# The opening of an attention and mixer kernel, rebuilt: v loaded straight into its rows, one head's scores by the ordinary product, two AV products moved among the scores

## The chip, the cores and the metric

The kernel runs on one core of a Trainium2 chip. The metric is device time in microseconds (us), the median of several runs. The core's engines each run their own list of instructions in order and wait for one another by semaphores: PE (matrix products; its weight loads are shown as PEld), DVE (VectorE), ACT (ScalarE), POOL (GpSimd) and SP (SyncE). POOL and SP issue the DMA transfers here: POOL those that also change float32 to bfloat16, SP the rest.

## The reference

q, k and v have shape 8 batches x 8 heads x 576 positions x 64, s has 8 x 8 x 576. Each head is causal attention with a bias from the running sum of the positive part of s; its output x then goes through a low-rank mixer over positions (U, V of rank 32) and a two-layer mixer over channels.

```python
scores = scale * np.matmul(q, k.transpose(0, 1, 3, 2))
cum = np.cumsum(np.maximum(s, 0.0), axis=-1)
bias = -(cum[:, :, :, None] - cum[:, :, None, :])
scores = np.where(causal, -1e9, scores + np.minimum(bias, 0.0))
attn = np.exp(scores - np.max(scores, axis=-1, keepdims=True))
attn = attn / (np.sum(attn, axis=-1, keepdims=True) + 1e-09)
x = np.matmul(attn, v)          # then heads side by side: 8 x 576 x 512
u = x + (x.T @ U @ V).T         # per batch, over positions
out = u + np.maximum(u @ w_ch1, 0.0) @ w_ch2
```

## The kernel before

**Units of work.** Heads go in pairs: 32 pairs, four to a batch. A pair has these steps, each a Python generator whose pieces the order written at the end of the kernel calls one by one with `step`:

- `transposes(n)`, T: PE turns q and k of both heads (`q_sd`, `k_sd`) into PSUM tiles (L317); `copies` (L291) says for each head and half whether ACT or DVE copies them into `slot` (L340), where head and position stand crosswise. A slot has 64 rows of q or k and four rows more, the bias rows, which a DMA on SP fills (L233 for batch 0, L301 later): the cumulative sum in three bfloat16 parts, and ones. So one product of slot with slot gives score plus bias.
- `scores(n)`, S: for each head a "near" tile of 128x1024 (six matmuls, L404) and one exponential on ACT (L419) into `pT`; then one "mid" tile for both heads (L430) and one small "tail" tile (L436). The near, mid and tail pieces together are the causal half of the 576x576 scores. PSUM holds two such large tiles (`pscore`) and four of 128x512 (`pwork`).
- masks on the diagonal blocks: in batch 0 POOL does three for each pair (L152).
- `values(n)`, V (AV): 15 matmuls for each head (L464) with v from `v_slot`, whose 65th column of ones gives the sum of each row, then on DVE a reciprocal (L473) and a product (L474) into `x_sb`.
- `mix_first`, M: the low-rank mixer of batch 0, for each of four blocks of 128 channels: five matmuls with `U_sb` (L598), DVE copy to `ux_first` (L601), then four transposing matmuls and one with `V_sb` (L605, L613), ACT to `uT` (L621). Then comes the first channel product (L650), with the first half of w1.

**The first batch.** Two things are special at the start. First, near scores of pair 0 do not wait for the bias rows in slot 0: `near_by_rows` (L358) builds score and bias in PSUM from the row tile itself with 27 matmuls on 64 rows (L366), in four pieces, and does it for both heads (generators `A` and `B_`). Second, batch 0's v comes as one DMA in long runs, four positions to a partition (`v_raw`, L167, 512 KB in bfloat16), and `v_tiles` (L575) brings it into order by 16 matmuls with a selecting matrix `sel` and four DVE casts (L590); the last 64 positions come straight (L188). `spin` (L216) issues matmuls on a constant tile whose result nobody reads; they keep PE at work.

**What sets the order.** PE and POOL run in the order in which the kernel is written; so do DVE, ACT and SP up to the end of batch 0 (`in_program_order`). POOL's DMA issues share eight semaphores in turn, so an issue waits for the landing of the eighth before it, and the queue carries them in the order of issue. The order of the opening stands in lines 1098 to 1168: spins, T0, A, T1, pieces of `B_` between T2, then S0, T3, S1, masks, S2 with `v_tiles` inside, S3 with V0 in its midst, V1, M, V2, M, V3, M.

On POOL the order is: q and k of batch 0 in four pieces each, `sel`, `keep` (a constant mask used from batch 1 on), v, memsets of `v_slot`, the end of v, memsets of U_sb and V_sb, U, U, V (L262 to L266), first half of w1 (L270), masks of pair 0, first four heads of batch 1's q and k, memsets of the ones in pT, masks of pair 1, second half of w1, and so on.

Of the kernel before, what the change touches and what calls it, by code (L numbers as in the profile page):

```python
# [39 lines left out]
def kernel(  # L40
# [52 lines left out]

    PW = 1664
    v_early = work.tile([128, NF, 512], BF16, tag="hT", name="hT").rearrange("p a b -> p (a b)")
    v_raw = v_early[:, 0:2048].rearrange("p (h t d) -> p h t d", h=H, t=4)
# [27 lines left out]
    def ones(ap):  # L124
# [10 lines left out]
    load_qk(0, 4, 2)  # L135
    load_qk(0, 6, 2)

    sel = consts.tile([128, 516], BF16)
    nc.vector.memset(sel, 0.0)
    nc.gpsimd.affine_select(  # L140
        out=sel,
        in_=sel,
        compare_op=ALU.not_equal,
        fill=1.0,
        base=-3,
        pattern=[[1, 516]],
        channel_multiplier=-4,
    )
# [16 lines left out]
    nc.gpsimd.memset(keep, 3.0e38)  # L165
    causal(keep, 1, 128)
    nc.gpsimd.dma_start(  # L167
        out=v_raw.rearrange("p h t d -> p h (t d)"),
        in_=v[0, :, 0:512, :].rearrange("h (p t) d -> p h (t d)", t=4),
    )  # L170

    v_slots = [consts.tile([128, 5, H, D + 1], BF16, name=f"v_slot{i}") for i in range(3)]

    def init_v(eng, vt):
# [6 lines left out]

    def load_v(b, parts=range(5)):
        vt = v_slot(b)
        if b < 3:
            init_v(nc.gpsimd, vt)
        for t in parts:
            rows_t = 128 if t < 4 else 64
            nc.gpsimd.dma_start(  # L188
                out=vt[:rows_t, t, :, 0:D],
                in_=v[b, :, ds(t * 128, rows_t), :].rearrange("h p d -> p h d"),  # L190
            )

    load_v(0, [4])
    nc.gpsimd.memset(U_sb, 0.0)
    nc.gpsimd.memset(V_sb, 0.0)

    pTs = [consts.tile([128, 2, PW], BF16, name=f"pT{i}") for i in range(2)]

# [12 lines left out]

    for slot in slots:
        nc.vector.memset(slot[:KA, :, 2 * S :], 0.0)


    def spin(n, dst):  # L216
# [12 lines left out]
    nc.vector.tensor_copy(rows[:, 1, 1, :], rest)  # L229
    nc.vector.tensor_sub(rows[:, 2, 1, :], rest, rows[:, 1, 1, :])  # L230
    for n in range(PB):
        for hh in range(2):
            nc.sync.dma_start(  # L233
                out=slots[n][D:KA, hh, 0 : 2 * S],
                in_=rows[2 * n + hh : 2 * n + hh + 1].rearrange("n r c s -> n r (c s)"),
            )
# [16 lines left out]
    def weight_sums():  # L253
        for dst, a, b in ((B_1, B12, B11), (B_2, B22, B_1), (B_4, B21, B_2), (B_3, B22, B12)):
            for k4 in range(0, HF, 4):
# [6 lines left out]
    nc.gpsimd.dma_start(  # L262
        out=U_sb[:, :4, 0:R], in_=moe_U[:512].rearrange("(kt kp) r -> kp kt r", kp=128)
    )
    nc.gpsimd.dma_start(out=U_sb[:64, 4, 0:R], in_=moe_U[512:576])
    nc.gpsimd.dma_start(out=V_sb[:R], in_=moe_V)  # L266
    w1_in = moe_w_ch1.rearrange("(kt kp) n -> kp kt n", kp=128)

    def load_w1(half):
        nc.gpsimd.dma_start(  # L270
            out=w1_sb[:, :, ds(half * 1024, 1024)], in_=w1_in[:, :, ds(half * 1024, 1024)]
        )
# [5 lines left out]
        )  # L278

    load_w1(0)  # L280
    alloc_qk(1)
    uT_of, x_of, xT_of = {}, {}, {}

# [6 lines left out]

    def copies(n, hh, par):  # L291
        b = n // PB
        on_act = hh == (n == 4) and ((n in (0, 1, 4, 8, 9) or n > 8 and n % PB == 2) or n == 2 and par == 0)
        return nc.scalar.copy if on_act else nc.vector.tensor_copy

    def transposes(n):
        b, hp = divmod(n, PB)
        slot = slot_of(n)
        if b > 0:
            for r, n_r, c in ((0, 3, 1), (3, 1, 0)):  # L300
                nc.sync.dma_start(  # L301
                    out=slot[ds(D + r, n_r), :, ds(c * S, S)],
                    in_=rows_hbm[ds(r, n_r), ds(2 * n, 2)],
                )
        tps = {}

        def turn(hh, c):
            if c == 0:
                tile = pwork()
                if (n, hh) == (3, 0):  # L310
                    spin(2, tile)
                tps[hh] = tile.bitcast(BF16)[:, : 2 * 4 * TP].rearrange(
                    "p (c t m) -> p c t m", c=2, t=4
                )
            src = (q_t[b], k_t[b])[c]
            for t2 in range(4):
                nc.tensor.transpose(  # L317
                    tps[hh][:, c, t2, :],
                    src[:, 2 * hp + hh, ds(t2 * 128, 128)],
                    identity[:TP, :TP],  # L320
                )

        if b == 0:
            for hh in range(2):
                turn(hh, 0)
            yield
        for hh in range(2):
            if b > 0:
                turn(hh, 0)
            turn(hh, 1)  # L330
            tp = tps[hh]
            dst = slot[0:D, hh, 0 : 2 * S]
            for par in range(2):
                src = tp[par * D : par * D + D]
                if in_runs(b, 2 * hp):
                    by_run = dst.rearrange("p (c t two m) -> p c t two m", c=2, t=4, two=2)
                    copies(n, hh, par)(by_run[:, :, :, par, :], src)  # L337
                else:
                    in_turn = dst.rearrange("p (c m t two) -> p c m t two", c=2, t=4, two=2)
                    copies(n, hh, par)(  # L340
                        in_turn[:, :, :, :, par], src.rearrange("p c t m -> p c m t")
                    )
            yield
# [53 lines left out]
        nc.scalar.activation(pT[:, hh, 0:1024], near, EXP, scale=scale)  # L397
        yield

    def scores(n, pT, spins=()):  # L400
        slot = slot_of(n)

        def mm(dst, hh, j, lo, hi):
# [5 lines left out]
                stop=True,  # L409
            )  # L410

        tail = None
        for hh in range(2) if n > 0 else ():
            near = pscore()
            for j in range(4):
                mm(near[:, ds(j * 128, 128)], hh, j, j * 128, j * 128 + 128)
            mm(near[:, 512:960], hh, 0, 128, S)
            mm(near[:, 960:1024], hh, 3, 512, S)
            nc.scalar.activation(pT[:, hh, 0:1024], near, EXP, scale=scale)  # L419
            if n >= PB:  # L420
                mask(pT[:, hh, 0:512].rearrange("p (a b) -> p a b", a=4), 4, 128)
            if spins:
                tail = tail or pwork()
                spin(spins[hh], tail)
            yield
        mid, tail = pscore(), tail or pwork()
# [144 lines left out]
        evac(slice(0, 4), 512, S, ut)  # L571
        yield


    def v_tiles():  # L575
        vt = v_slots[0]
        pvs = [pwork() for _ in range(4)]
        spin(2, pvs[0])
        yield
        for t in range(4):  # L580
            for j, pv in enumerate(pvs):
                nc.tensor.matmul(
                    pv.rearrange("p (h d) -> p h d", h=H),
                    lhsT=sel[ds(32 * j, 32), ds(3 + 128 * j - t, 128)],
                    rhs=v_raw[ds(32 * j, 32), :, t, :],
                    start=(t == 0),
                    stop=(t == 3),
                )
        for j, pv in enumerate(pvs):
            nc.vector.tensor_copy(vt[:, j, :, 0:D], pv.rearrange("p (h d) -> p h d", h=H))  # L590

    ux_first = work.tile([128, PB, 128], BF16, tag="ux_first", name="ux_first", bufs=1)

# [496 lines left out]
    def step(*gens):  # L1090
        for gen in gens:
            next(gen, None)
# [2 lines left out]
        spin(n, (ps or pscore)()[:, 0:512])  # L1095

    act, dve = nc.scalar.copy, nc.vector.tensor_copy
    S0, S1, S2, S3 = (scores(n, pT_of(n), {1: (2, 3), 3: (2, 0)}.get(n, ())) for n in range(PB))
    T0, T1, T2, T3 = (transposes(n) for n in range(PB))
    M0, M1, M2, M3 = (mix_first(dt, act) for dt in range(PB))  # L1100
    A, B_ = (near_by_rows(hh, pT_of(0)) for hh in range(2))
    spin_some(9)
    step(T0)
    spin_some(2)
    step(T0, T0)
    step(A, A, A, A)
    step(T1, T1, T1)
    step(B_)
    step(T2)
    step(B_)  # L1110
    step(T2, T2)
    step(B_, B_)
    step(S0, S0)
# [201 lines left out]
```

## Time and profile before

| what | value |
|---|---|
| time, median of 3 runs | 363.95 us (363.31 to 364.02) |
| span of the profiled execution | 362.1 us |
| time less that span | 1.85 us |
| PE busy | 350.2 us (97%) |
| DVE busy | 276.5 us (76%) |
| ACT busy | 213.0 us (59%) |
| POOL busy | 84.7 us (23%) |
| first 30 us: PE, DVE, ACT, POOL busy | 27.30, 23.51, 19.34, 27.09 us |
| chain that ended last: PE, DVE, ACT, DMA | 76%, 11%, 4%, 4% |

A line such as "13.54 1.02 ACT L397 ..." in a timeline has start and length in us, engine, line of the kernel, operation, tiles, shape and count; brackets tell how long the engine was idle before and what ended it. The chain that ended last is followed back from the end; in order of time it lists start, length and what ran. A DMA row ends with the us from issue to landing. The stages list for each stretch the busy time of PE, PEld, DVE, ACT and POOL, the granted clock of PE as a share, the busy share of the DMA engines (over 1 where several transfers overlap on an engine) and GB/s.

### The profile page before, as it was taken

To read this page: it belongs to the slowest core of one execution; us is meant where nothing else is said; L and a number is where in the kernel's file an instruction comes from. 1 tells how busy PE (TensorE), PEld (TensorE's weight loads), DVE (VectorE), ACT (ScalarE), POOL (GpSimd) and SP (SyncE) were. 2 spreads that over 40 slices of the span, in tenths; PEclk is the share of its full clock that TensorE was granted. 3 is DMA by queue.
4 is the path that set the end of the run, shared out by engine and by line. 5 is a ranking of instruction groups with operands and counts; after the bars stand their busy time and mean duration, and the time that the engine had idled before them with its cause. 6 is when DMAs were issued, how large, how long until landed. Compare 5 with 4: busy or idle time off the path is not lost.

```text
span 362.1 us, 9616 instructions
## 1 busy us (share of the span) xinstructions
PE 350.2 (97%) x3999; PEld 256.7 (71%) x4039; DVE 276.5 (76%) x605; ACT 213.0 (59%) x322; POOL 84.7 (23%) x108
## 2 busy tenths in 40 slices
PE   8999999999998999999999999999899999999996
PEld 3676566665587667876688667876488548888885
DVE  8776776778788758995699659986697769676674
ACT  3875975846761678347843676348743554675710
POOL 8997261714040403140214013000000000000000
PEclk9999999999999999999999999999999999999999
DMA  7999999999999899969994999255022716010022
GB/s 104 169 198 204 150 174 129 152 150 143 98 109 114 147 121 70 97 94 126 128 91 72 127 150 91 51 123 79 4 38 70 143 24 125 29 60 31 30 89 87
DMA packets 155123, 37.94 MB, mean 105 GB/s; under 512 B 138696, under 2 KB 153448, under 8 KB 155080
## 3 DMA queue, kind: packets, MB, share of 16 engines
q0 software_dynamic: 110016, 18.50, 82.6%
q1 hardware_dynamic: 44776, 18.64, 31.4%
q8 instruction: 31, 0.51, 0.6%
q10 hardware_dynamic: 288, 0.20, 0.2%
q14 instruction: 12, 0.10, 0.1%
HBM read 37.25 MB, written 9.70 MB: 130 GB/s over the span
## 4 chain that ended last, share of the span: by engine, by line
PE 76%; DVE 11%; ACT 4%; DMA 4%; issue 3%; POOL 1%; DVEq 0%; ACTq 0%; POOLq 0%
PE pwork L650 21%; PE pwork L699 11%; PE pscore L404 9%; PE quarter L699 9%; PE pwork L464 7%; PE parts L929 6%; PE pwork L317 4%; PE pwork L660 3%; DMA xT<-x_sb 2%; DVE slot L677 2%; DVE uT L518 2%; ACT hT L1018 2%; DVE o_sb L713 2%; DMA k_sd<-in_k_dram 2%; ACT pT L419 1%
## 5 line engine op out<-in xcount | busy, mean ns | idle before, releaser
L650 PE MATMUL pwork<-uT,w_sb 128*128 128x512 bf16 x401 | 105.9, 379 | 2.6 <-ACT hT L1018 0.9
L1018 ACT ACTIVATE hT<-pwork 128x512 bf16<-128x512 f32 x108 | 65.2, 608 | 38.4 <-PE pwork L650 38.2
L419 ACT ACTIVATE pT<-pscore 128x1024 bf16<-128x1024 f32 x56 | 56.5, 1029 | 49.8 <-PE pscore L404 49.0
L650 PEld LDWEIGHTS <-w_sb 128*128 128x128 bf16 x448 | 38.3, 98 | 35.9 <-issue 1.3
L404 PE MATMUL pscore<-slot 68*128 68x320 bf16 (+1 forms) x500 | 55.2, 246 | 0.2
L404 PEld LDWEIGHTS <-slot 68*128 68x128 bf16 x564 | 41.2, 97 | 16.9 <-issue 1.3
L699 PEld LDWEIGHTS <-hT 128*128 128x128 bf16 x496 | 46.3, 98 | 7.0 <-DVE uT L518 0.5
L188 POOL DMA_DIRECT2D v_slot<-in_v_dram x36 | 30.3, 855 | 77.6 <-PE pwork L464 65.9
L349 DVE TENSOR_TENSOR pT<-pT,keep 128x512 bf16<-128x512 bf16 (+1 forms) x81 | 28.6, 354 | 21.8 <-ACT pT L419 16.0
L337 DVE COPY slot<-pwork 64x576 bf16<-64x576 bf16 x76 | 34.4, 453 | 4.6 <-PE pwork L317 3.7
L464 PEld LDWEIGHTS <-pT 128*128 128x128 bf16 x870 | 32.4, 98 | 6.9 <-issue 1.8
L464 PE MATMUL pwork<-v_slot,pT 128*128 128x65 bf16 x870 | 35.5, 193 | 1.2 <-DVE uT L518 1.2
L474 DVE TENSOR_TENSOR x_sb<-pwork,rec 128x320 bf16<-128x320 f32 x64 | 31.2, 488 | 1.4
L430 ACT ACTIVATE pT<-pscore 128x1024 bf16<-128x1024 f32 x29 | 30.2, 1043 | 1.7 <-PE pscore L404 1.5
L699 PE MATMUL pwork<-w_sb,hT 128*128 128x256 bf16 x240 | 30.6, 273 | 0.0
L340 DVE COPY slot<-pwork 64x576 bf16<-64x576 bf16 x29 | 23.3, 802 | 5.4 <-PE pwork L317 3.6
L699 PEld LDWEIGHTS <-slot 128*128 128x128 bf16 x256 | 24.1, 98 | 4.6 <-issue 1.6
L114 POOL DMA_DIRECT2D q_sd<-in_q_dram x6 | 12.6, 2105 | 47.2 <-PE pwork L317 34.5
L473 DVE RECIPROCAL rec<-pwork 128x5 f32<-128x5 f32 x64 | 12.0, 190 | 12.3 <-PE pwork L464 12.1
L699 PE MATMUL pwork<-w_sum,slot 128*128 128x256 bf16 x160 | 20.3, 272 | 0.7 <-DVE o_sb L713 0.7
L317 PEld LDWEIGHTS <-q_sd 72*128 72x128 bf16 x256 | 14.7, 98 | 8.8 <-DMA q_sd<-in_q_dram 1.0
L699 PE MATMUL quarter<-w_sb,hT 128*128 128x256 bf16 x144 | 18.0, 273 | 0.3 <-DVE uT L518 0.3
(165 smaller groups left out, 544.4 us busy)
## 6 DMA issues: line engine op xcount, KB each, us to landing
out_dram<-o_sb SPq DMA_DIRECT2D x34, 256.0 KB
w_sb<-in_moe_w_ch_dram POOLq DMA_DIRECT2D x4, 1024.0 KB, 14.3
v_slot<-in_v_dram POOLq DMA_DIRECT2D x28, 128.0 KB, 8.3
q_sd<-in_q_dram POOLq DMA_DIRECT2D x5, 576.0 KB, 15.6
k_sd<-in_k_dram POOLq DMA_DIRECT2D x5, 576.0 KB, 21.8
q_sd<-in_q_dram POOLq DMA_DIRECT2D x4, 288.0 KB, 13.2
k_sd<-in_k_dram POOLq DMA_DIRECT2D x4, 288.0 KB, 13.5
q_sd<-in_q_dram POOLq DMA_DIRECT2D x4, 144.0 KB, 5.2
```

What stands on the lines that cost most here:

```text
L188: nc.gpsimd.dma_start(out=vt[:rows_t, t, :, 0:D], in_=v[b, :, ds(t * 128, rows_t), :].rearrange("h p d -> p h d"),)
L317: nc.tensor.transpose(tps[hh][:, c, t2, :], src[:, 2 * hp + hh, ds(t2 * 128, 128)], identity[:TP, :TP],)
L337: copies(n, hh, par)(by_run[:, :, :, par, :], src)
L349: nc.vector.tensor_tensor(dst, dst, keep[:, :, 0:w].to_broadcast([128, n_tiles, w]), op=ALU.min)
L404: nc.tensor.matmul(dst, lhsT=slot[0:KA, hh, ds(S + j * 128, 128)], rhs=slot[0:KA, hh, lo:hi], start=True, stop=True,)
L419: nc.scalar.activation(pT[:, hh, 0:1024], near, EXP, scale=scale)
L430: nc.scalar.activation(pT[:, :, 1024:1536], mid.rearrange("p (a b) -> p a b", a=2), EXP, scale=scale)
L464: nc.tensor.matmul(po[:, i, :], lhsT=pT[:, hh, ds(place(j, i), 128)], rhs=vt[:, j, h, :], start=(j == 0), stop=(j == i), skip_group_check= ...
L474: nc.vector.tensor_tensor(x_sb[:, hp, :, ds(hh * D, D)], po[:, :, 0:D], rec.to_broadcast([128, 5, D]), op=ALU.mult,)
L650: nc.tensor.matmul(f1, lhsT=w1_sb[:, kt, ds(nf * 128, 128)], rhs=u[:, kt, :], start=(kt == 0), stop=(kt == 3),)
L699: nc.tensor.matmul(acc[:, i, :], lhsT=a[:, kt, ds(i * 128, 128)], rhs=b[:, kt, :], start=(begin and i == 0 and kt == 0), stop=(kt == HF - ...
L1018: nc.scalar.activation(hT[:, nf, :], f1, RELU)
```

## The change

- Batch 0's v is loaded like every other batch's: five DMAs straight into `v_slot` (four of 128 positions and one of 64, runs of 64 numbers). `v_raw`, `sel` and `v_tiles` go. The memsets of this v slot move from POOL to DVE.
- `near_by_rows` is kept for the first head of pair 0. The second head's near scores come from `scores(0)`, by six matmuls on slot 0 with its bias rows; the DMA of these rows is issued before that of the first head's.
- U, U and V of the mixer and the mask `keep` are issued after the masks of pair 0 (`load_mixers`), behind the first half of w1; memsets of U_sb, V_sb and of the ones in pT stand between w1 and the masks. The first q and k of batch 1 come after the masks of pair 1.
- The order: S0's three pieces directly after T1, T2 after it in one go; T3 in three pieces between S1, S2 and V0; V0 inside S2, V1 and the first M piece inside S3.
- One of two copies of pair 1's first head goes to DVE, and the one of pair 2 on ACT too. Spins stay in two places only: at the start and two ahead of S0.

```diff
-    nc.gpsimd.dma_start(
-        out=v_raw.rearrange("p h t d -> p h (t d)"),
-        in_=v[0, :, 0:512, :].rearrange("h (p t) d -> p h (t d)", t=4),
-    )
...
-        if b < 3:
+        if 0 < b < 3:
             init_v(nc.gpsimd, vt)
...
-    load_v(0, [4])
-    nc.gpsimd.memset(U_sb, 0.0)
-    nc.gpsimd.memset(V_sb, 0.0)
...
+    init_v(nc.vector, v_slots[0])
+    load_v(0)
...
-        for hh in range(2):
+        for hh in (1, 0) if n == 0 else range(2):
             nc.sync.dma_start(
                 out=slots[n][D:KA, hh, 0 : 2 * S],
...
     load_w1(0)
+    for pT in (*pTs, pT_early[0]):
+        nc.gpsimd.memset(pT[:, :, 1600:], 1.0)
+    nc.gpsimd.memset(U_sb, 0.0)
+    nc.gpsimd.memset(V_sb, 0.0)
+
+    def load_mixers():
+        nc.gpsimd.dma_start(
+            out=U_sb[:, :4, 0:R], in_=moe_U[:512].rearrange("(kt kp) r -> kp kt r", kp=128)
+        )
+        nc.gpsimd.dma_start(out=U_sb[:64, 4, 0:R], in_=moe_U[512:576])
+        nc.gpsimd.dma_start(out=V_sb[:R], in_=moe_V)
+        nc.gpsimd.memset(keep, 3.0e38)
+        causal(keep, 1, 128)
...
-        on_act = hh == (n == 4) and ((n in (0, 1, 4, 8, 9) or n > 8 and n % PB == 2) or n == 2 and par == 0)
+        on_act = hh == (n == 4) and (
+            n in (0, 4, 8, 9) or n > 8 and n % PB == 2 or n == 1 and par == 0
+        )
...
-        for hh in range(2) if n > 0 else ():
+        for hh in range(n == 0, 2):
             near = pscore()
+            spin(spins[hh], near[:, 0:512])
...
     step(A, A, A, A)
     step(T1, T1, T1)
-    step(B_)
-    step(T2)
-    step(B_)
-    step(T2, T2)
-    step(B_, B_)
-    step(S0, S0)
-    step(T3, T3, T3)
-    step(S1)
+    step(S0, S0, S0)
     masks(pT_of(0), True)
-    load_qk(1, 0, 4)
-    for pT in (*pTs, pT_early[0]):
-        nc.gpsimd.memset(pT[:, :, 1600:], 1.0)
-    step(S1)
+    load_mixers()
+    step(T2, T2, T2)
+    step(S1, S1)
+    step(T3)
+    step(T3)
     step(S1, S1)
     masks(pT_of(1), True)
+    load_qk(1, 0, 4)
     nc.gpsimd.memset(slots[PB][D:KA, :, 0 : 2 * S].bitcast(mybir.dt.uint32), 0x3F803F80)
     load_w1(1)
-    step(S2)
-    vs = v_tiles()
-    step(vs)
-    step(S2)
-    drain(vs)
-    step(S2)
-    step(S3)
-    step(S2)
+    step(S2, S2)
+    step(V0, V0)
+    step(T3)
+    step(S2, S2)
     masks(pT_of(2), True)
     nc.gpsimd.memset(pT_early[1][:, :, 1600:], 1.0)
     step(S3)
-    drain(values(0, pT_of(0)))
+    step(V1, V1)
+    step(S3)
+    step(M0)
     step(S3, S3)
     masks(pT_of(3), True)
-    drain(values(1, pT_of(1)))
     load_qk(1, 4, 4)
     load_w2(0)
     nc.gpsimd.memset(V_end, 0.0)
-    step(M0)
-    drain(values(2, pT_of(2)))
+    step(V2, V2)
     step(M0, M1)
-    drain(values(3, pT_of(3)))
+    step(V3, V3)
     step(M1, M2)
```

More of the change, by code (lines that the diff above doesn't have):

```diff
@@ L95 @@
     v_early = work.tile([128, NF, 512], BF16, tag="hT", name="hT").rearrange("p a b -> p (a b)")
-    v_raw = v_early[:, 0:2048].rearrange("p (h t d) -> p h t d", h=H, t=4)
     pT_early = [
@@ L136 @@
     load_qk(0, 6, 2)
[L138 to L147, printed above, removed]
-    )
     keep = consts.tile([128, 1, 128], BF16)
@@ L164 @@
     V_end = consts.tile([128, 4, 64], BF16)
-    nc.gpsimd.memset(keep, 3.0e38)
-    causal(keep, 1, 128)
-    nc.gpsimd.dma_start(
-        out=v_raw.rearrange("p h t d -> p h (t d)"),
-        in_=v[0, :, 0:512, :].rearrange("h (p t) d -> p h (t d)", t=4),
-    )
     v_slots = [consts.tile([128, 5, H, D + 1], BF16, name=f"v_slot{i}") for i in range(3)]
@@ L261, in weight_sums @@
                 yield
[L262 to L266, printed above, removed]
     w1_in = moe_w_ch1.rearrange("(kt kp) n -> kp kt n", kp=128)
@@ L309, in turn @@
                 tile = pwork()
-                if (n, hh) == (3, 0):
-                    spin(2, tile)
                 tps[hh] = tile.bitcast(BF16)[:, : 2 * 4 * TP].rearrange(
@@ L398, in near_by_rows, with scores @@
         yield
-    def scores(n, pT, spins=()):
+    def scores(n, pT, spins=(0, 0)):
         slot = slot_of(n)
@@ L410, in mm @@
             )
-        tail = None
-        for hh in range(2) if n > 0 else ():
+        for hh in range(n == 0, 2):
             near = pscore()
+            spin(spins[hh], near[:, 0:512])
             for j in range(4):
@@ L421, in scores @@
                 mask(pT[:, hh, 0:512].rearrange("p (a b) -> p a b", a=4), 4, 128)
-            if spins:
-                tail = tail or pwork()
-                spin(spins[hh], tail)
             yield
-        mid, tail = pscore(), tail or pwork()
+        mid, tail = pscore(), pwork()
         for hh in range(2):
@@ L572, in seqmix @@
         yield
[L575 to L590, printed above, removed]
     ux_first = work.tile([128, PB, 128], BF16, tag="ux_first", name="ux_first", bufs=1)
@@ L1097 @@
     act, dve = nc.scalar.copy, nc.vector.tensor_copy
-    S0, S1, S2, S3 = (scores(n, pT_of(n), {1: (2, 3), 3: (2, 0)}.get(n, ())) for n in range(PB))
+    S0, S1, S2, S3 = (scores(n, pT_of(n), {0: (0, 2)}.get(n, (0, 0))) for n in range(PB))
     T0, T1, T2, T3 = (transposes(n) for n in range(PB))
     M0, M1, M2, M3 = (mix_first(dt, act) for dt in range(PB))
-    A, B_ = (near_by_rows(hh, pT_of(0)) for hh in range(2))
+    A = near_by_rows(0, pT_of(0))
+    V0, V1, V2, V3 = (values(n, pT_of(n)) for n in range(PB))
     spin_some(9)
```

## The prediction

> **What bounds it now.** I read the slices first, then the chain of waits of the opening, its stages, the timeline of each engine, and last the landings. The page's slices have PE at 9 or more nearly everywhere from the second on: what is won in the opening reaches the end if the work behind it stays the same. The chain of the first 50 us, in order of time (start, length, what; lines left out):
>
> ```profile
> 4.16 5.60 DMA k_sd<-in_k_dram
> ...
> 9.80 0.43 PE pwork L317 x8
> ...
> 13.51 0.56 PE pscore L404 x4
> ...
> 17.93 1.03 ACT pT L430
> ...
> 19.61 0.97 PE pwork L582 x16
> ...
> 21.17 1.03 ACT hT L430
> ...
> 24.46 0.91 PE pwork L464 x30
> ...
> 25.68 1.07 PE pwork L464 x30
> ...
> 27.46 0.95 PE pwork L464 x29
> ...
> 28.68 0.20 PE pwork L464
> ```
>
> Until 9.8 the second pair's k sets the pace. From 13.5 to 22 PE and the exponentials on ACT alternate. From 22.2 PE alone runs: AV of four pairs (L464), 1 us each. My marker is the last AV matmul, at 28.68. The stages say the same (PE, PEld, DVE, ACT, POOL busy; clock; DMA share; GB/s):
>
> ```profile
> 12.00:20.00 8.00, 7.63 (x94) 4.98 (x97) 5.64 (x7) 6.91 (x10) 8.00 (x16) 1.00 1.31 178
> 20.00:29.00 9.00, 8.46 (x176) 6.96 (x171) 7.41 (x21) 5.76 (x9) 8.17 (x16) 1.00 1.15 204
> ```
>
> ACT's timeline gives the pitch of the exponentials, and the point that the change can bring forward (13.54):
>
> ```profile
> 10.18 1.60 ACT L340 COPY slot<-pwork 64x576 bf16<-64x576 bf16 x2
> ...
> 13.54 1.02 ACT L397 ACTIVATE pT<-pscore 128x1024 bf16<-128x1024 f32 x1 [0.33 <-PE pscore L366]
> 14.46 1.02 ACT L430 ACTIVATE pT<-pscore 128x1024 bf16<-128x1024 f32 x1
> 15.37 0.28 ACT L436 ACTIVATE pT<-pwork 128x128 bf16<-128x128 f32 x1
> ```
>
> Starts are 0.92 apart, 0.17 after the small one. The DMA share is over 1 from 5 us on, so POOL's queue is full. Issues with the time to landing, of the k loads, of v as it is now, and of later v loads in the new form (128 KB each):
>
> ```profile
> k_sd<-in_k_dram POOLq DMA_DIRECT2D x1, 144.0 KB, 5.8
> ...
> hT<-in_v_dram POOLq DMA_DIRECT2D x1, 512.0 KB, 8.1
> ...
> v_slot<-in_v_dram POOLq DMA_DIRECT2D x1, 64.0 KB, 6.6
> ...
> w_sb<-in_moe_w_ch_dram POOLq DMA_DIRECT2D x1, 1024.0 KB, 10.3
> ...
> v_slot<-in_v_dram POOLq DMA_DIRECT2D x1, 128.0 KB, 5.2
> ...
> v_slot<-in_v_dram POOLq DMA_DIRECT2D x1, 128.0 KB, 5.8
> ```
>
> With their issue times: the last k lands at 6.88+5.8 = 12.7, v at 9.04+8.1 = 17.1, its end at 17.7, U at 18.5 and 18.9, V at 19.2, the first half of w1 at 14.71+10.3 = 25.0. Landings keep the order of issue, so the queue is one line.
>
> **The sum's basis.** The profiled execution spans 362.1 us; the median of the runs shown is 363.95 (363.31 to 364.02), so 1.85 lies around the span. I change the opening and keep the 1.85.
>
> **PE: taken out.** The rows product of the second head (27 matmuls, L366; four stretches, 0.45 for the first three, some 0.4 for each six, 0.45 at the end: about 2.2 us), the v permutation (16 matmuls, 0.97) and eleven filler matmuls (L218, 0.22 each: 2.4). Added: six score matmuls (0.45) and two fillers (0.43). That is 4.7 us less PE work, but PE has no claim on it before 22 us, since other things release it there.
>
> **The score of the second head.** The ordinary product needs the four bias rows in slot 0. SP issues them from 8.20, now this head first. Bounds: the load of s, on the same queue, took 2.65 us from issue to use (0.81 to 3.46), so 10.85; the middle scores read these rows at 13.44 without waiting, so 13.4. The trace's semaphore updates lie between: 12.2 and 12.4 for the first two issues, 13.8 and 15.6 for the next. I take those; nothing that SP's queue holds changes but the swap. PE is through with pair 1's transposes at 10.23 and its two fillers at 10.67, waits until 12.25, and the exponential starts at 12.25+0.64 = 12.9 instead of 13.54 (0.64 is the start-to-start of L404 14.90 to ACT 15.54). Then 13.8, 14.7, and pair 1's first at 14.9 (15.54 before). Pair 1's second head waits for its rows: PE 15.7 (before 16.20), ACT 16.3 (16.84). So ACT gains 0.5 here, and at most that, until rows come sooner.
>
> **PE's clock in that gap.** 1.6 us of idle PE is new; the longest wait of before is under half a microsecond, and every row has the clock at 1.00. Bounds: nothing, or half speed for the 1.9 us of scores and transposes that follow (0.95 of pair 0's scores, 0.52 of transposes, 0.45). Half speed would cost 1.9, of which the waits up to 15.7 (1.2) take the most. I take nothing: the row nearest to it is a wait that changed no clock. [...]
>
> **Copies.** One of pair 1's and one of pair 2's leave ACT for DVE: 0.80 each. ACT's 10.18 copy is now one, DVE's chain runs 11.0 to 13.4 (pair 1), 13.8 to 17.0 (pair 2), 17.0 to 18.7 (pair 3, first head). The scores that read them come at 14.0, 15.7, 17.4, 18.3, so all are covered, by 0.6 us or more. The four casts of v (2.49) vanish from DVE. The three memsets of the v slot move from POOL, where they take 0.53, 0.24, 0.21, to DVE ahead of s; on DVE between 0.43 (0.27 as the like-sized sel memset, twice 0.08 as the slot memsets) and 0.98. Room: 0.40 idle before L223 plus 0.27 of the sel memset gone. So 0 to 0.3 late; I take 0, since DVE's own rows are nearest.
>
> **AV among the scores.** V0 (30 matmuls, 1.0) comes after pair 2's second near score, at 18.8; before, at 22.68. It needs v (below, 18.1 at the latest part, the fifth tile) and pair 0's masks. POOL does those at 14.3 to 15.9, ahead of its U loads. Behind V0 on PE wait the last transposes of pair 3, and on DVE two reciprocals and two products (0.2 and 0.49 each, 1.5 with gaps) go before pair 3's last two copies, which end at 22.6. So pair 3's second near score starts at 22.65, 0.4 later than now: the new tight spot. From there, if nothing else waits: its exponential at 23.6 (0.92 after the one before), the middle at 24.5, the small one 25.4 to 25.7, POOL's mask to 26.1; PE meanwhile does M0, the rest of S3, V2, M0/M1 up to 26.2; V3 ends at 27.2. Against 28.68: a gain of 1.5. That is the most I can find.
>
> **U, moved behind w1.** U and V were issued at 12.9 to 14.7, ahead of w1. Now POOL issues v in five parts (0.89 each, 7.6 to 11.8), w1 (11.8), five memsets, three masks, and then U, U, V at 15.9 to 17.8, so U stands behind 1 MB. M0 is moved ahead of S3's middle scores and needs both parts of U; PE is in order, so S3's rest, V2, M1, V3 all wait behind it, and ACT too. Landing: 12.7 (last k) + v + w1 + U. v: the later loads land 1.6, 1.1, 1.3 apart (220.5, 222.1, 223.2, 224.5 for 216.02+4.5, 216.91+5.2, 217.79+5.4, 218.66+5.8) and 1.4, 1.0, 1.9 apart at 46 to 50, where transposing DMAs share the engines. Bounds 1.0 and 1.9; I take 1.2, nearest to the undisturbed ones, for 4.5 loads 5.4 (now 5.0: 12.7 to 17.7). w1: 5.85 (19.16 to 25.0), 5.4 for its second half (28.5 to 33.9); 4.9 and 6.3 are the extremes of w2. I take 5.4. U's two parts: 0.8 and 0.3. Sum: 12.7+5.4+5.4+1.1 = 24.6, bounds 23.2 and 28.7. From U's landing PE has: one matmul 0.06, S3's rest 0.50, V2 0.94, M0/M1 0.72, V3 1.0: 3.2. V3 ends at 27.8, against 28.7: **0.9 gained**. U before 24.0 costs nothing; the break-even is 25.4.
>
> [...]
>
> **Other moves.** The first q/k of batch 1 are issued at 19.8 instead of 16.9, behind pair 1's masks, but follow V's landing in the same line: about 28.4, as now (28.5), and their readers start at 34.27. w1's second half goes out at 22.3 (21.36), the second q/k at 27.4 (25.93), w2 at 28.8 (27.35): all of them now sit 12 to 16 us in the queue, which covers 1.5. keep is made later and is read after 39 us. The order from V3 on is as before, so the 0.9 carries to the end.
>
> **Rivals.**
> (1) U is no wait: landing by 24.0, if v goes at 1.1 and w1 at 4.9 or 5.2. Time 363.95−1.5 = 362.4. For it: the 222.1 to 223.2 interval. Against: w1 took 5.85 here.
> (2) The gain dissolves: U near 25.4, or behind 30 us PE meets something that does not move, such as the DMA transposes near 105 (one took 8.67 on the chain). PE is idle for 1.45 us between 100 and 140, so up to that can be lost. 363.9.
> (3) Slower: v's small packets take the line longer, U lands after 26.2, PE stops at M0 with ACT behind it. That is the point from which it counts: 1.6 per load (7.2, U at 26.4) gives 1.0 lost, 365.0; 1.9 and 6.3 give 3.3, 367.2. For it: the 1.6 and 1.9 among the rows.
>
> **Numbers.** A change of less than 0.2% (0.73 us) cannot be told from none. Chances: U between 24.0 and 25.2, a gain of 0.2 to 1.5 around 0.9, 0.42, of it 0.28 past the bound; (1) 0.18; (2) 0.13; (3) 0.27. Faster 0.46, same 0.27, slower 0.27. The forecast is 363.95−0.9 = 363.1 (its own range 362.5 to 363.8). The range goes from 362.1 (rival 1, with bias rows 0.3 sooner) to 365.4 (v at 1.7).
>
> **What would show it.** Right: ACT's second exponential near 12.9; first AV matmul near 18.8; M0's first weights waiting for U, landing near 24.6; last AV matmul of pair 3 near 27.8; later rows all sooner by that. Wrong: M0 waiting past 26, AV waiting for v, bias rows landing later than 16, clock under 1.00 after 10.7, or a marker that is sooner while the end is not.

## The result: 1.0% slower, because PE's clock fell

The changed kernel takes 367.31 us (median of 6 executions, 366.18 to 368.51), the kernel before 363.63 beside it (362.20 to 364.51). The ratio is 1.0104, 95% interval 1.0079 to 1.0128. Forecast were 363.1 us and a range of 362.1 to 365.4: the time lies outside it, and on the other side of the kernel before. Here and below, medians are over all executions, while a ratio with its interval leaves out the slow ones (over 1.5% above the fastest of the same kernel) and is not the quotient of the medians.

The profiled execution spans 365.7 us and took 367.46, so 1.8 lies around the span. The page of the changed kernel says first that something new is there, in its slices: the row of the granted clock has a stretch at half speed.

```profile
span 365.7 us, 9529 instructions
...
PEclk9658999999999999999999999999999999999999
```

In the page of before all these digits were 9. The stages of the opening (columns as before: PE, PEld, DVE, ACT, POOL busy; clock; DMA share; GB/s), first the two that were shown of before, then cut where the clock changes:

```profile
12.00:20.00 8.00, 6.36 (x61) 5.18 (x62) 4.92 (x7) 4.16 (x6) 6.37 (x15) 0.54 2.06 178
20.00:29.00 9.00, 8.85 (x102) 7.47 (x101) 5.77 (x13) 5.91 (x8) 6.76 (x12) 0.50 1.07 163
9.23:12.64 3.41, 0.97 (x17) 0.57 (x16) 2.00 (x4) 1.69 (x2) 3.41 (x6) 1.00 1.57 160
12.64:29.71 17.07, 15.92 (x168) 13.24 (x169) 10.11 (x18) 10.42 (x14) 12.89 (x27) 0.50 1.49 172
29.71:33.00 3.29, 3.24 (x80) 3.00 (x79) 2.54 (x9) 1.91 (x4) 2.37 (x5) 1.00 1.05 192
```

From 20 to 29 us PE ran 102 matmuls at 0.50 where the kernel before ran 176 at 1.00. The clock is 1.00 until 12.64, 0.50 for exactly 17.07 us, and 1.00 again from 29.71. The chain of the first 45 us (start, length, what) has the same steps as predicted, at other times:

```profile
8.15 5.35 DMA slot<-hT
13.50 0.14 issue
13.64 1.86 PE pscore L392 x10
...
21.98 1.65 PE pwork L449 x30
...
25.68 1.65 PE pwork L449 x30
...
29.68 0.98 PE pwork L449 x30
...
31.38 0.91 PE pwork L449 x30
```

PE waits for pair 0's bias rows until 13.5. AV of pairs 0 and 1 (L449) takes 1.65 each, where such pieces took 0.91 to 1.07 before. My marker, the last AV matmul of pair 3, comes at 32.1; it was 28.68, and 27.8 was forecast. ACT's timeline has the exponential of pair 0's second head at 14.69 (before 13.54, forecast 12.9):

```profile
10.14 0.78 ACT L328 COPY slot<-pwork 64x576 bf16<-64x576 bf16 x1
14.69 1.02 ACT L407 ACTIVATE pT<-pscore 128x1024 bf16<-128x1024 f32 x1 [3.77 <-PE pscore L392]
15.61 1.02 ACT L415 ACTIVATE pT<-pscore 128x1024 bf16<-128x1024 f32 x1
```

The loss is made before 30 us and then carried: the first transposes of batch 1 start at 37.69 (before 34.27, 3.4 later), the 400th recorded matmul of the channel product's first line at 295.3 (291.6), the span ends 3.6 later.

### The profile page after: what moved, and what is told of

It reads as the page before. It is cut to its first block, busy times and chain, and to the rows that moved or that the text cites. A ratio compares the mean times of both kernels' runs of the same rounds, so it can differ in the third digit from the quotient of the medians.

```text
span 365.7 us, 9529 instructions
## 1 busy us (share of the span) xinstructions
PE 351.4 (96%) x3954; PEld 259.6 (71%) x3993; DVE 275.5 (75%) x605; ACT 211.7 (58%) x320; POOL 86.0 (24%) x107
## 4 chain that ended last, share of the span: by engine, by line
PE 79%; DVE 9%; ACT 4%; DMA 4%; issue 2%; DVEq 0%; ACTq 0%
PE pwork L618 21%; PE pwork L667 11%; PE pscore L392 10%; PE quarter L667 10%; PE pwork L449 7%; PE parts L897 6%; PE pwork L305 4%; PE pwork L628 3%; DMA xT<-x_sb 2%; DVE uT L503 2%; DVE slot L645 2%; ACT hT L986 2%; DMA slot<-hT 1%; ACT pT L407 1%; PE pscore L197 1%
## 5 line engine op out<-in xcount | busy, mean ns | idle before, releaser
L407 ACT ACTIVATE pT<-pscore 128x1024 bf16<-128x1024 f32 x57 | 57.4, 1029 | 54.1 <-PE pscore L392 53.3
L392 PE MATMUL pscore<-slot 68*128 68x128 bf16 (+1 forms) x506 | 60.1, 259 | 3.6 <-DMA slot<-hT 3.3
L392 PEld LDWEIGHTS <-slot 68*128 68x128 bf16 x570 | 44.4, 103 | 20.0 <-DVE slot L328 3.5
L169 POOL DMA_DIRECT2D v_slot<-in_v_dram x40 | 33.8, 866 | 78.5 <-PE pwork L449 68.5
L449 PEld LDWEIGHTS <-pT 128*128 128x128 bf16 x870 | 33.9, 100 | 7.3 <-issue 2.0
L449 PE MATMUL pwork<-v_slot,pT 128*128 128x65 bf16 x870 | 36.8, 197 | 1.3 <-DVE uT L503 1.3
L325 DVE COPY slot<-pwork 64x576 bf16<-64x576 bf16 x76 | 34.4, 453 | 4.6 <-PE pwork L305 3.7
L415 ACT ACTIVATE pT<-pscore 128x1024 bf16<-128x1024 f32 x29 | 30.2, 1041 | 2.1 <-PE pscore L392 2.0
L328 DVE COPY slot<-pwork 64x576 bf16<-64x576 bf16 x31 | 24.8, 801 | 8.0 <-PE pwork L305 6.2
L305 PE MATMUL pwork<-identity,k_sd 72*128 72x72 bf16 x256 | 18.6, 201 | 0.1
## 6 DMA issues: line engine op xcount, KB each, us to landing
k_sd<-in_k_dram POOLq DMA_DIRECT2D x4, 288.0 KB, 10.9
```

The costliest lines, as they stand in the source:

```text
L169: nc.gpsimd.dma_start(out=vt[:rows_t, t, :, 0:D], in_=v[b, :, ds(t * 128, rows_t), :].rearrange("h p d -> p h d"),)
L305: nc.tensor.transpose(tps[hh][:, c, t2, :], src[:, 2 * hp + hh, ds(t2 * 128, 128)], identity[:TP, :TP],)
L392: nc.tensor.matmul(dst, lhsT=slot[0:KA, hh, ds(S + j * 128, 128)], rhs=slot[0:KA, hh, lo:hi], start=True, stop=True,)
L415: nc.scalar.activation(pT[:, :, 1024:1536], mid.rearrange("p (a b) -> p a b", a=2), EXP, scale=scale)
L449: nc.tensor.matmul(po[:, i, :], lhsT=pT[:, hh, ds(place(j, i), 128)], rhs=vt[:, j, h, :], start=(j == 0), stop=(j == i), skip_group_check= ...
```

## The experiments

In the result the clock is one suspect of three. PE had been idle for 3.29 us (10.35 to 13.64) when it fell, so the first theory was: an idle stretch of about 3.3 us lets the clock fall. The rivals: the late bias rows cost the time by themselves, or U behind w1 does.

### Fillers in the idle stretch, 15 and 7 of them

```diff
-    S0, S1, S2, S3 = (scores(n, pT_of(n), {0: (0, 2)}.get(n, (0, 0))) for n in range(PB))
+    S0, S1, S2, S3 = (scores(n, pT_of(n), {0: (0, 15)}.get(n, (0, 0))) for n in range(PB))
```

> The changed kernel, with 15 filler matmuls instead of 2 ahead of pair 0's score piece (13 times 0.22 us, about 2.9 us of PE work in a stretch in which it had been idle for 3.29 us). Clock theory (the idle stretch makes the clock fall to half for 17 us, and that is what the change loses): granted clock 1.00 throughout, pair 0's score piece still near 13.6 because its rows still land at 13.5, first AV matmul near 19, last AV of pair 3 begins near 28, time 362.5 to 363.8, ratio to before about 0.998. Waiting theory (late bias rows alone cost the 3.6 us): nothing changes but the fillers, time 367. U theory (U behind the first half of w1 holds PE): PE stops at the first mixer piece until 24.8, ratio over 1.003.

Measured: 366.07 us beside 363.1, ratio 1.0062 (1.0021 to 1.0103). The fillers did fill the stretch: PE was busy for 3.34 of the 3.40 us from 10.6 to 14.0. The clock stayed up there, and fell later, at 17.61, for 10.24 us. Of 12 executions 10 had a mean granted clock under 0.997. I count these as executions with a fall: one stretch of 3.41 us at half clock lowers the mean over the span by 0.005.

> The changed kernel with 7 fillers instead of 2 ahead of pair 0's score piece: the idle stretch is about 2.1 us instead of 3.3. Clock theory with a threshold above 2 us: clock 1.00 and the time of the run with 15 fillers, 362.5 to 363.8. Clock theory with a threshold below 2 us: clock half for some 17 us, about 367. Waiting theory: 367.

The same line with `(0, 7)`. Measured: 367.99, ratio 1.0073 (1.0028 to 1.0118); the clock fell in all 12 executions, in the profiled one at 15.68, after an idle stretch of only 1.52 us. So the idle theory was wrong in its form, and the run with 15 fillers missed its 362.5 to 363.8.

### The rows product put back, and v's new load alone

```diff
-        for hh in range(n == 0, 2):
+        for hh in range(2) if n > 0 else ():
...
-    A = near_by_rows(0, pT_of(0))
+    A, B_ = (near_by_rows(hh, pT_of(0)) for hh in range(2))
...
-    step(S0, S0, S0)
+    step(B_)
+    step(T2)
+    step(B_)
+    step(T2, T2)
+    step(B_, B_)
+    step(S0, S0)
...
```

The bias rows of pair 0 go back to their old order as well.

> The changed kernel, with the second head's near scores of pair 0 by the rows product again, in pieces among pair 2's transposes as in the kernel before; v straight, U behind w1 and AV among the scores stay. Clock theory: PE has no idle stretch over about 1.3 us, the clock stays at 1.00, time 363 to 364.3. Waiting theory (late rows alone): also sooner than 367, since pair 0's first exponential of the second head needs no rows, but the clock may be anything: 365 to 366. U theory: the same wait as in the changed kernel, over 365.

Measured: 365.24, ratio 1.0063 (1.0018 to 1.0108). No idle stretch was longer than 0.6 us, and yet the clock fell in all 12 executions, in the profiled one at 14.92.

The next one takes the kernel before and gives it v's direct load alone: `v_raw`, `sel`, `v_tiles` and its fillers go, `load_v(0)` comes in place of `load_v(0, [4])`.

> The kernel before, with one part of the change: batch 0's v by five loads straight into its rows; the selecting product with its four casts, its constant and two of the fillers are gone. Order of all else as before. If v's small packets delay the bias rows: these rows land 1.3 to 2 us later than in the kernel before (13.5 and 14.0 for the first two instead of 12.2 and 12.4), although the rows product keeps PE at work until about 14. Clock theory: no long idle stretch, clock 1.00, time 363.5 to 364.3. If v's form itself costs the 3.6 us: 366 to 367.

Measured: 364.85, ratio 1.0051 (1.0026 to 1.0075), the clock fell in 8 of 12. The four executions at full clock took 362.68 to 364.91, so v's form by itself is not the 3.6 us. The first two bias rows land at 12.97 and 13.16, 0.8 us later than before and sooner than expected. Its profiled execution is the one that overthrew the idle theory. The stages up to the fall and behind it:

```profile
5.63:9.04 3.41, 3.35 (x43) 2.08 (x40) 3.29 (x6) 2.12 (x3) 3.22 (x8) 1.00 1.13 147
9.04:12.46 3.42, 3.29 (x53) 2.34 (x52) 2.10 (x3) 2.74 (x4) 3.16 (x6) 1.00 1.30 159
12.46:26.11 13.65, 13.40 (x83) 8.26 (x81) 5.61 (x7) 9.17 (x12) 12.52 (x23) 0.50 1.43 169
```

PE was busy for 3.29 of 3.42 us just before the clock fell to half, and for 13.40 of 13.65 us while it stayed there. Busy time is not what the clock follows.

### What it follows: a sum over stretches of 3.41 us

Each half-speed time in the five profiles so far is a whole number of 3.413 us (3, 4 or 5: 10.24 us with 15 fillers, 13.65 with the rows product back, 17.07 in the changed kernel), and each starts a whole number of them after the first full clock (in the changed kernel 6.83 us, two of them). So I cut each trace into these stretches and summed, for each, what the matmuls streamed: columns times time for a column (in the changed kernel's chain four products of 512 columns take 0.86 us at full clock, so 0.42 ns for a column; six score products with 1024 columns together take 0.44 there and 0.85 at half clock, so about twice that), weighted by the share of the 128 rows that the product uses. By the shapes in the timelines a filler uses 128 rows, a score 68, a transpose 72, the rows product 64, v's selecting product 32. Over the stretch that is the share of the 128 rows at work. The sums (a few matmul records lack, so some 0.02 can be missing):

| profile | share of the last stretch before the fall | lowest share that kept the clock |
|---|---|---|
| before | no fall | 0.37 |
| changed kernel | 0.13 | 0.48 |
| 15 fillers | 0.31 | 0.54 |
| 7 fillers | 0.29 | 0.48 |
| rows product back | 0.31 | 0.43 |
| v alone | 0.37 | 0.49 |

At half clock the stretches that did not bring it back had 0.38 to 0.74, those that did 0.746 or 0.747 (four profiles) and 0.81. Over these and all the later profiles, up to 340 us, nine falls came after 0.09 to 0.370, and every stretch that kept the clock had 0.368 or more, so the two touch at one point; seven returns to full speed from an opening came after 0.745 to 0.81, one after 0.857, one near 116 us after 0.99, and none of the stretches up to 0.740 returned. Counted by time alone, without the rows, no mark separates them: falls come after shares as high as 0.71, 0.80 and 0.96, while 0.44 kept the clock. This was found after the fact, so the next runs test it.

### The test: the same instructions on fewer rows

The kernel before with one change: its eleven later fillers read 32 rows of `busy` and not 128. Columns, count, order and waits stay, and nobody reads their result.

```diff
-    def spin(n, dst):
+    def spin(n, dst, k=32):
...
-                dst, lhsT=busy[:, 0:128], rhs=busy[:, 0 : dst.shape[1]], start=True, stop=True
+                dst, lhsT=busy[:k, 0:128], rhs=busy[:k, 0 : dst.shape[1]], start=True, stop=True
...
-        spin(n, (ps or pscore)()[:, 0:512])
+        spin(n, (ps or pscore)()[:, 0:512], 128)
```

> The kernel before with one thing changed: its eleven later fillers use 32 rows of the array instead of 128. Instructions, order, waits and PE's busy time stay. Density theory: the lowest share between 13 and 16.5 us goes from 0.45 to 0.32, so the clock falls in half of the runs or more (in the kernel before, in 5 of 35), median 365 to 367, and the profile, if it is one of these, has half clock from about 16 us on. Idle theory, and the theory that fillers do nothing: as before, 363.1, no more than 2 of 12 runs with a fall.

Measured: 368.84 us (6 executions, 366.59 to 370.84) beside 363.39, ratio 1.0134 (1.0082 to 1.0186). The clock fell in all six; in the kernel before, over the 101 executions taken beside the experiments, it fell in 15. The median is 2 us over what was expected, since the fall took up to six stretches. The stages of this run:

```profile
12.13:15.54 3.41, 3.36 (x45) 2.30 (x44) 2.54 (x4) 2.98 (x5) 3.41 (x6) 1.00 1.28 162
15.54:18.95 3.41, 3.36 (x25) 1.50 (x24) 3.08 (x4) 2.98 (x4) 3.41 (x10) 1.00 1.33 196
18.95:22.37 3.42, 3.39 (x25) 1.41 (x25) 0.52 (x1) 2.09 (x3) 3.30 (x7) 0.50 1.12 211
```

and of the kernel before at the same place:

```profile
15.45:18.86 3.41, 3.15 (x27) 1.86 (x25) 3.32 (x5) 3.07 (x6) 3.41 (x10) 1.00 1.25 167
18.86:22.27 3.41, 3.16 (x37) 1.73 (x37) 1.82 (x4) 3.20 (x6) 3.29 (x7) 1.00 1.07 196
```

With thin fillers PE was busier (3.36 against 3.15 us), and lost the clock. By hand: the stretch from 15.5 to 19 holds seven fillers of 0.215 us and score pieces of about 3 x 1024 + 128 columns, 1.35 us on 68 of 128 rows, 0.72. With full fillers that is (1.51 + 0.72) / 3.41 = 0.65, with thin ones (0.38 + 0.72) / 3.41 = 0.32.

The same from the other side, the 15 fillers of the first run on 32 rows (`spin` has the parameter `k` here too, 128 where nothing is said):

```diff
-            spin(spins[hh], near[:, 0:512])
+            spin(spins[hh], near[:, 0:512], 32)
```

> The run with 15 fillers, but these fillers use 32 of the 128 rows of the array instead of all 128: the same count, the same columns, the same time on PE, a quarter of the cells at work. Density theory (what the clock follows is the share of the array's cells at work in a stretch of 3.41 us; it falls to half after a stretch under some 0.37, and comes back after one over some 0.745): with these fillers the stretch from 10 to 13.5 has a share near 0.19, so the clock falls there in every run and stays half until about 30 as in the changed kernel: granted clock 0.977 in the profile, time 366.5 to 368. Idle theory (PE must have instructions to run, of whatever kind): no difference from the run with full fillers, clock 0.986 or over, fall not before 16 us, 365 to 366.5.

Measured: 368.72 (6 executions), ratio 1.0109 (1.0051 to 1.0167), a fall in all six. The profiled one lost the clock at 14.03, after a share of 0.27, where the run with full fillers had 0.76. It got it back after three stretches, sooner than expected, and took 365.09; four of the others were at half clock for five or six. In the timelines of PE the two runs differ by the filler's shape; thin:

```profile
10.34 3.41 PE L197 MATMUL pscore<-busy 32*128 32x512 bf16 x15
13.68 1.60 PE L392 MATMUL pscore<-slot 68*128 68x128 bf16 x10
```

and full:

```profile
9.57 3.40 PE L197 MATMUL pscore<-busy 128*128 128x512 bf16 x15
13.04 1.04 PE L392 MATMUL pscore<-slot 68*128 68x128 bf16 x10
```

The fillers last as long in both, and the scores behind them run at 1.60 for ten against 1.04.

### The clock kept, and a second obstacle

Three more full fillers where the share had been 0.31:

```diff
+            if more[hh]:
+                tail = tail or pwork()
+                spin(more[hh], tail)
             yield
-        mid, tail = pscore(), pwork()
+        mid, tail = pscore(), tail or pwork()
...
-    ... scores(n, pT_of(n), {0: (0, 15)}.get(n, (0, 0)))
+    ... scores(n, pT_of(n), {0: (0, 15)}.get(n, (0, 0)), {1: (2, 1)}.get(n, (0, 0)))
```

> The run with 15 fillers, with three more full fillers behind pair 1's near score pieces (two and one), where its stretch from 14.2 to 17.6 had a share of 0.31. Density theory: the lowest share of any stretch is now about 0.40 to 0.45, the clock stays at 1.00 in most runs, first AV matmul near 18.8, time 362.2 to 363.2, ratio to before 0.997 to 1.000. Theory that the loss is something else than the clock: 365 to 367.

Measured: 365.56, ratio 1.0054 (1.0024 to 1.0085), a miss. The opening of the profiled execution does what was expected: no fall, lowest share 0.44, the first transposes of batch 1 at 33.54 (before 34.27). It loses the clock at 116.54 instead, for one stretch, after PE had stood still for 2.93 us from 113.4; in 8 of the 12 executions the mean clock shows a fall, of one stretch in six of them. The next run has POOL's order of the kernel before as well:

```diff
     init_v(nc.vector, v_slots[0])
+    nc.gpsimd.memset(keep, 3.0e38)
+    causal(keep, 1, 128)
+    nc.gpsimd.memset(U_sb, 0.0)
+    nc.gpsimd.memset(V_sb, 0.0)
     load_v(0)
+    nc.gpsimd.dma_start(
+        out=U_sb[:, :4, 0:R], in_=moe_U[:512].rearrange("(kt kp) r -> kp kt r", kp=128)
+    )
...
-    load_mixers()
```

> The run before it, with the order on POOL as in the kernel before: the two memsets and keep ahead of v, so v is issued about 1.8 us later and the bias rows of the first pairs pass ahead of it (13.0, 13.2, 13.6, 14.3 for the first four instead of 13.0, 13.4, 14.4, 15.2), and U, U and V ahead of the first half of w1 (landing near 19.5 instead of 24). If the clock stays at 1.00: 0 to 0.4 us better than the run before it, 362.0 to 363.0. If it falls, 365 or more.

Measured: 366.13, ratio 1.0042 (1.0003 to 1.0080), a miss too. Again the opening is better than before, the first transposes of batch 1 at 32.01, 2.26 us sooner; the bias rows land at 12.03, 12.26, 12.74 and 13.43. Of this lead 0.96 is left at 104, and none at 113. The chain there, of this run:

```profile
103.37 0.85 DVE x_sb L461 x2
104.22 0.03 DVE o_sb L683
104.25 10.87 DMA xT<-x_sb
115.12 0.02 issue
115.15 0.56 DVE uT L505
```

and of the kernel before:

```profile
104.33 0.85 DVE x_sb L474 x2
105.21 8.67 DMA xT<-x_sb
113.90 0.56 DVE uT L518
```

The last DMA transpose of batch 2 was issued 0.96 sooner and landed 1.24 later. PE's longest wait there:

```profile
PE pwork L451 <- DVE uT L505: 3.4, 1, 3.4
```

(columns: who waited for whom, us in total, times, longest), against 1.2 in the kernel before. An idle stretch of 3.36 us is also one of low share (PE was busy for 0.20 of the 3 us from 113), and in 7 of 12 executions of this run the mean clock shows one stretch at half or so. Beside the transpose, five v loads of batch 4 were issued (102.45 to 106.67), though batch 4's v is first read at 153.4, some 47 us later. The next four runs hold them back: a small memset on columns of `xT` that nobody reads makes POOL wait for the transpose.

```diff
         if hp == 0 and 2 <= b < B - 1:
+            if b == 3:
+                nc.gpsimd.memset(xT_of[2][:, PB - 1, S:], 0.0)
             load_v(b + 1)
```

> The run with v later and U sooner, and in it batch 4's five v loads (issued at 102.5 to 106 there) held on POOL by a small memset until the last DMA transpose of batch 2 has landed (issued 104.25, landed 115.12, PE idle for 3.3 us). If these loads are what slows that transpose: it lands within 7 us of its issue, PE's idle stretch near 113 goes, the clock has no fall there, and the 2.26 us that the opening won (first transposes of batch 1 at 32.0 instead of 34.3) reach the end: 361.0 to 362.0, ratio to before 0.995. If the transpose waits for what was issued before it (batch 3's k, 110.66): nothing changes at 115, 363.5 to 366.

Measured: 361.45 us (9 executions, 361.05 to 364.92) beside 363.27, no fall in any of the nine. The medians stand as 0.995; the ratio with its interval is 0.9981 (0.9954 to 1.0007), since four of the nine lie between 362.4 and 364.9. The time is what was expected, though the interval still touches 1. The page and POOL's timeline:

```profile
span 359.6 us, 9560 instructions
...
PEclk9999999999999999999999999999999999999999
```

```profile
111.39 0.16 POOL L1206 MEMSET xT<- 128x64 bf16 x1 [21.51 <-DMA xT<-x_sb]
112.01 4.22 POOL L169 DMA_DIRECT2D v_slot<-in_v_dram  x5 [0.46 <-PE pwork L550]
```

The transpose, issued at 103.7, landed at 111.34: 7.6 us instead of 10.9, a little over the 7 expected. PE's wait there fell to 0.2 us, from 3.4:

```profile
PE pwork L451 <- DVE uT L505: 0.2, 1, 0.2
```

> The kernel before with the same hold alone. Its transpose takes 8.67 us (105.21 to 113.9) and PE is idle there for about 0.9 us. If the v loads slow it: 0.8 to 1.0 us faster, 362.2 to 362.5. If not: 363.1 to 363.4.

Measured: 362.94 beside 363.27, ratio 1.0025 (0.9988 to 1.0062), with a fall in 3 of 12. The idle stretch at 113 is gone, but the 0.8 to 1.0 us expected are not seen beyond the scatter. In this kernel the hold shows no gain.

> The changed kernel with the hold on batch 4's v alone, and the change's two fillers. Clock theory: the opening still loses 3.4 us to the half clock; the hold can take away no more than the 1.0 us of PE idle near 117: 366.0 to 367.3. If the hold is what mends the runs before it, and not the fillers: 361 to 363.

Measured: 365.92, ratio 1.0044 (1.0011 to 1.0077), a fall in all 12; the profiled one from 12.56 to 29.63. The hold alone does not mend the opening.

> The changed kernel with 15 and three more fillers and the hold on batch 4's v, but with the change's own order on POOL: U behind the first half of w1 (it landed at 24.1 to 24.8 in the runs so far, and PE waited 0.4 us for it once the clock stayed at 1.00). If U's place is worth little: first transposes of batch 1 at 32.8 to 33.6, 361.5 to 362.5. If U's place decides: 363 or more.

Measured: 362.82 beside 363.37, ratio 0.9966 (0.9930 to 1.0001); 2 of 12 executions show a fall of one stretch. U landed at 24.55 and 24.74, the last AV matmul of pair 3 started at 27.9, the first transposes of batch 1 at 33.52. The 361.5 to 362.5 was missed by 0.3. The run with POOL's old order took 361.45, with these transposes at 32.76. What U's place alone costs is not shown: that run issues v later too, and the same opening without the hold had them at 32.01.

This run and the one before it differ by the sixteen added fillers alone. The stretch in which the clock was at half, first with two fillers, then with eighteen:

```profile
12.56:29.63 17.07, 15.75 (x165) 13.11 (x166) 10.22 (x19) 10.31 (x13) 12.82 (x27) 0.50 1.60 169
12.56:29.63 17.07, 15.00 (x257) 11.68 (x256) 13.24 (x29) 12.64 (x17) 15.78 (x32) 1.00 1.64 181
```

The first transposes of batch 1 start at 37.70 and at 33.52, and the medians are 365.92 and 362.82. So it is the fillers that mend the opening: adding work for PE made the kernel 3.1 us faster.

What the hold does is seen in four pairs of profiles that differ by it alone. The transpose takes 10.87 us without it and 7.6 with it (POOL's old order), 10.45 and 7.6 (this run, and the same without the hold: issued at 104.45 and 104.46), 8.9 and 4.9 (the change's two fillers), 8.7 and 3.2 (the kernel before). Of the second pair, the chain without the hold, and POOL's memset that waits for the transpose:

```profile
104.45 10.45 DMA xT<-x_sb
```

```profile
112.10 0.16 POOL L1209 MEMSET xT<- 128x64 bf16 x1 [22.74 <-DMA xT<-x_sb]
```

## Why the prediction was wrong, step by step

**PE's removed work: what led to the failing step.** The prediction counted eleven fillers among what PE sheds and said that PE has no claim on that time. As time, that holds. But the fillers were the only products on all 128 rows before AV starts at 22.7 us, and what is left in the opening (68, 72 and 64 rows) can't, by the count of rows, reach a share over 0.56 even when PE never waits. Thinning these same eleven fillers costs the kernel before 5.4 us in the median (368.84 against 363.39), with no instruction removed.

**"PE's clock in that gap": the failing step.** The prediction put this term at nothing. Measured, the clock stood at half for 17.07 us, after a stretch with a share of 0.13. Against the same kernel with sixteen more fillers, which kept the clock there, this cost 4.15 us at the first transposes of batch 1 (37.69 against 33.54). Of the two bounds, none or half speed for 1.9 us of work, the second was itself too small: the clock stayed half for 17.07 us, since the scores and AV that follow at half clock have shares of 0.39 to 0.72, and in no profile did a share up to 0.740 bring it back. The row that I rested on, a wait under half a microsecond that changed no clock, was the wrong sort of row: the stretch around it (5.2 to 8.6 us) still had a share of 0.45. That PE's busy time does not decide was shown by the run with v alone: a stretch with PE busy for 3.29 of 3.42 us lost the clock, and 13.65 us with PE busy for 13.40 did not bring it back.

**The bias rows.** Taken: 12.2 and 12.4 for the first two, inside bounds of 10.85 and 13.4. Measured 13.50 and 14.01, outside. "Nothing that SP's queue holds changes" was true and not enough: the v loads were issued at 7.6 to 11.8, and from 12 to 14 us the DMA share was 2.77 where it had been 1.32 before, which is the likely reason. In the eight profiles with v issued from 7.6 on, the third row lands at 14.1 to 15.4; in the three with v from 9.3 on at 12.7 to 13.5. Together with the sooner end of PE's work this made the gap 3.29 and not 1.6. By itself it costs little: with the clock kept, the first transposes of batch 1 come sooner than before all the same.

**v, w1 and U.** Forecast 5.4 for v, 5.4 for w1, U at 24.6. Measured: v 12.79 to 19.16, 6.4; w1 5.2, until 24.37; U's two parts 0.5 instead of 1.1, at 24.84. The errors cancelled, so that U's landing came out right was luck. For v the ten other profiles with five loads had 5.4 to 6.5, so the 5.4 that I took was their lower end, and this run lies near the upper.

**AV among the scores, and the gain.** Nearly right, as the runs with the clock kept show: first AV forecast at 18.8, measured 18.8 in one and 19.6 to 19.9 in three; last AV of pair 3 with U behind w1 forecast at 27.8, measured 27.9 there; without U's wait forecast at 27.2, measured 27.2 and 26.4. So with the change's own order on POOL and the clock kept, the marker came within 0.1 us of its forecast, though the first AV came 0.9 later than planned and sixteen fillers were added.

**"The 0.9 carries to the end".** Half right. The loss of 3.4 carried (3.6 at the end). A gain need not: two runs led by 0.7 and 2.3 us at the first transposes of batch 1 and by 0.8 and 1.0 when batch 2's last DMA transpose was issued, and were 1.0 and 1.2 behind when it landed. Rival (2) named that place and the DMA transposes, at up to 1.45 us; it cost 1.8 and 2.2 there, since the transpose itself became slower.

**The rivals.** Rival (3), slower, was right in sign and wrong in cause: U landed before its break-even of 25.4. No rival had the clock in it, though "clock under 1.00 after 10.7" stood in the list of what would show the forecast wrong, and did.

**Open.** Whether the columns that a product's weights fill count beside its rows is untested: every product in the traces of both kernels has 128 of them (32*128 to 128*128). Whether the lower bound is 0.37 or a little more cannot be told, since some 0.02 may be missing from the sums. One execution of the changed kernel shows a mean clock of 1.00 at 368.51 us, and some at full clock in other runs lie up to 3.9 us over their fastest; that isn't explained. Why the transpose at 104 took 10.9 rather than 8.7 us when it was issued sooner is not known; holding the v loads made it shorter in both cases.

## What to carry to other kernels

Before filler products or wide auxiliary products are taken out, sum for every 3.41 us what share of the 128 rows the rest keeps at work: in these profiles 0.37 was the edge below which the clock fell to half, and it came back only from 0.745. Products on 64 to 72 rows, at most 0.56 by the count of rows, stay under the second mark, and come near the first even when PE waits little: in the kernel before the stretch from 8.6 to 12.0 us, with PE busy for 3.20 of 3.41, had 0.37. Here such a stretch kept its clock with fillers on all rows beside it, and the PE time that these take does not tell what they are worth: sixteen more brought 365.92 down to 362.82. A gain in an opening must also be followed to the next place where a transfer and not an engine sets the time; there, look which loads issued just then could wait.

## What the runs showed that I had not expected

- The clock followed how many rows the products use, not how busy PE is: equal instructions on 32 and on 128 rows made 368.84 and 363.39 us.
- The two marks lie far apart (0.37 and 0.745), so one thin stretch in the opening cost three to five stretches at half speed in the profiles, up to 17.07 us.
- The kernel before stands near the edge itself (0.37 at its lowest): in 15 of 101 executions its clock fell, and these took 366.0 to 368.8 us, the other 86 at most 364.8.
- Five loads of 64 to 128 KB, read some 47 us later, made a DMA transpose 2.9 to 5.5 us longer.
